# A fused adaLN block on one core: gate sums and weight preparation moved later, and the order of ScalarE and VectorE changed at the end of phase 1 and in the MLP's first pair

## The chip, the cores and the metric

The kernel runs on one core of a Trainium2 chip. The time is the device time of one execution in microseconds (us). The engines are named as in the profile: PE is TensorE's matmul, PEld its weight load, DVE VectorE, ACT ScalarE, POOL GpSimd, SP the engine that issues most loads and stores. A "phase" is a stage of the kernel, a "tile" 128 rows of x, a "pair" two tiles.

## The reference, cut to what matters

x has 2048 rows of 640 columns. Six vectors of 640 come from silu(c) @ w_mod.

```
mod = (_silu(c) @ w_mod).reshape(c.shape[0], 6, 1, -1)
sa, ca, ga, sb, cb, gb = (mod[:, 0], mod[:, 1], mod[:, 2], mod[:, 3], mod[:, 4], mod[:, 5])
h = _layernorm(x, axis=-1) * (1 + ca) + sa
x = x + ga * _A_ref(h, A_wqkv, A_w_phi, A_wo)
h = _layernorm(x, axis=-1) * (1 + cb) + sb
x = x + gb * _B_ref(h, B_w1, B_b1, B_w2, B_b2)
```

_A_ref is linear attention with 32 heads of 20 columns: q and k go through a small matrix per head and two softmaxes (of p and of -p), kv and z are sums of phi_k with v and with ones over all rows, the output is (phi_q kv) / (phi_q z) @ wo. _B_ref is relu(h @ w1 + b1)^2 @ w2 + b2 with 1728 hidden columns. All is float32.

## The kernel before, in words

Matrices are split into a high and a low part, and each product is three matmuls (high by high, high by low, low by high), so that nearly every tensor that PE reads needs a copy on ACT (the high part) and a subtraction on DVE (the low part).

**Phase 1** goes through 16 tiles of 128 rows, t = 0 to 15, in pairs j = t // 2. LayerNorm of a pair (ln_parts, L330) sums and squares on ACT, makes scale and bias on POOL, and scales x in place on ACT (L347: xb). t1 (L380) transposes scaled x on PE (ta, L356), applies 1 + ca and sa on ACT (hfa, L367), and splits the result into hT (high part ACT L368, low part DVE L87). proj (L393) multiplies hT with the weights of k, v or q into pk, pv, pq. spread (L424) takes each head's largest and smallest value on DVE (mx) and subtracts them, exps (L431) takes exponentials on ACT, k_norm (L435) sums a tile's heads on DVE (sk), inverts and scales; do_kv (L441) adds phi_k^T v up in PSUM (kvp). q_chain (L462) does the same for q: mxq, eq, the sums rs_q (L474), and a store of eq to DRAM (esp). A tile's steps end with SIDE[t] (L520), which spreads other preparation over the loop: the sums over the six gate vectors (stage, L311, loads a row block of w_mod, mac, L291, multiplies it with silu(c) and adds, four of the five with L295: wm), and prep_wo (L480), which loads the output weights, multiplies them by ga on DVE (rwo, L495) and splits them (wo, ACT L496, DVE L87).

In this loop (L697) PE's order is written by hand. The other engines' order comes from a scheduler, which may be told that an instruction goes behind another (issue_after). The last four tiles of q, and k and v of tiles 14 and 15, are postponed behind the loop; from there (L740 on) the order on PE, DVE, ACT and POOL is the order of the code, while SP's is still the scheduler's. mod_row (L324) adds the 128 partitions of a gate sum up with a matmul of ones (mr, L327) and copies it to all partitions (gb_b, L328). bb is b2 times gb. kvs, zb and kvd are copies of kvp, zb filled on ACT and DVE from matmuls z (L790).

**Phase 2** divides and projects. For each tile e_prod (L842) multiplies eq (read back from DRAM as el) with zb (scr), e_recip and e_scale make ezb on DVE; tr_e (L881) turns ezb on PE (te) and copies it on ACT (ept); num (L896) multiplies by kv; num_hi and num_lo copy the high part to ot, subtract it in PSUM with a negative identity, and copy the low part; do_wo multiplies by wo (pwo). Loads and stores go through SP's queue, in order, each waiting for its row of memory. Rows of 640 columns that are short-lived (loads of w_mod and wo, b2s, MLP weights) share five places, tag s1.

**The MLP** goes through eight pairs j and seven steps n, two blocks of hidden columns each: up makes relu(...)^2 in ft (ACT L1209, DVE L1210), split_a the parts ra (ACT L1233), down multiplies with w2 one step later (acc). The next pair's second LayerNorm is done in pieces (ln_pieces, L1438: sums L1443, squares L1448, POOL L1450 to L1452, scaling xm L1455), put in by layer at the steps that LN_AT0 names; prep converts weights (w, ACT L978, DVE L87) in between.

Of the kernel before, what the change touches and what calls it, by code (L numbers as in the profile page):

```python
# [17 lines left out]
D = 640  # L18
# [32 lines left out]
def kernel(  # L51
# [85 lines left out]
    def tp(name):  # L137
        return psA.tile([P, 512], F32, tag="tp", name=name)
# [179 lines left out]
    def mod_mac(part, *ks):  # L318
        for k, t in [(k, stage(part * D, k)) for k in ks]:
            with tc.issue_after(newest(ET_.DVE)):  # L320
                mac(t, t, k, MA.get(part))
            MA[part] = t

    def mod_row(part, dest, h):  # L324
        p = tp(f"mr{part}_{h}")
        c = slice(h * HALF, (h + 1) * HALF)
        nc.tensor.matmul(p[:, :HALF], ones, MA[part][:, c], start=True, stop=True)  # L327
        nc.scalar.activation(dest[:, c], p[:, :HALF], AF.Copy)  # L328
# [48 lines left out]
    def newest(engine):  # L377
        return next(i for i in reversed(nc.cur_bb.bb.instructions) if i.engine == engine)

    def t1(j, *ds, more=None):  # L380
        if 0 in ds:
            HT[j] = ht(f"hT{j}", j)
        p = tp(f"ta{j}_{ds[0]}")
        for k, d in enumerate(ds):
            t_in(XB[j], d, p[:, 256 * k : 256 * k + 256])
        if more:
            mod_turn(more[0], p[:, 256:], 4)
        for k, d in enumerate(ds):
            t_out(cols_a, HT[j], d, f"a{j}", p[:, 256 * k : 256 * k + 256])
        if more:  # L390
            mod_sum(*more)

# [111 lines left out]
    def biases():  # L504
        b2s.append(row("s1", "b2s"))
        nc.sync.dma_start(b2s[0], bass.AP(tensor=b2.tensor, offset=b2.offset, ap=[[0, P], [1, D]]))
        nc.sync.dma_start(b1_t, b1)

    def wo_weights(*gs):
        for g in gs:  # L510
            prep_wo(g, ga_b)
# [14 lines left out]
        7: lambda: mod_mac(2, 4),  # L526
        8: lambda: None,
        9: lambda: wo_weights(0, 1),
        10: lambda: wo_weights(2, 3),
        11: lambda: wo_weights(4, 5),  # L530
        12: lambda: (nc.vector.tensor_scalar(cols_b[:, 5:10], cols_b[:, 5:10], 1.0, None, op0=ALU.add), mod_mac(5, 0, 1, 2)),
        13: lambda: (mod_mac(5, 3, 4), biases()),
    }


# [161 lines left out]
    for t in range(2, NT - 2):  # L697
        j, i = divmod(t, 2)
        if i == 0 and j < NT // 2 - 2:
            load_x(j + 2)  # L700
        PK[t] = row("s2", f"k{t}")
        to_sb(proj("k", t), PK[t])
        if t == NT - 4:
            t1(j + 1, 0, 1)
        if t == 9:
            mod_row(2, ga_b, 1)
        norm = j + 1 if i == 0 and t < NT - 4 else j + 2 if t == NT - 5 else None
        if norm:
            parts = ln_parts(XB[norm], f"a{norm}")
            with tc.issue_after(newest(ET_.Activation)):  # L710
                next(parts)
        p = proj("v", t, (1, 0, lambda: t1(j + 1, 4)) if t == NT - 3 else None)
        if i == 0:
            do_kv(t - 2)
            do_kv(t - 1)
            if t in AFTER_KV:
                AFTER_KV[t]()
        v_out(t, p)
        if norm:
            next(parts)  # L720
        EK[t] = tok2("k", f"ek{t}")
        spread(PK[t], EK[t], f"k{t}")
        exps(EK[t])
        if norm:
            next(parts)
        if i and t < NT - 4:
            t1(j + 1, 2, 3)
        with tc.issue_after(newest(ET_.DVE)):
            k_norm(EK[t], t)
        if t < NT - POSTPONED:  # L730
            do_q(t, (1, 3, lambda: t1(j + 1, 4, more=LAST_COL.get(t))) if i else None)
            q_chain(t)
        if i == 0 and t < NT - 4:
            t1(j + 1, 0, 1)
        SIDE[t]()
# [14 lines left out]
        spread(PK[t], EK[t], f"k{t}")  # L750
    do_kv(ka - 2)
    do_kv(ka - 1)
    mod_row(5, gb_b, 0)
    exps(EK[ka])
    k_norm(EK[ka], ka)
    do_q(q0)
    mod_row(5, gb_b, 1)
    exps(EK[kb])
    k_norm(EK[kb], kb)
    do_v(ka)  # L760
    q_chain(q0, False)
    do_v(kb)
    exps(EQ[q0])
    nc.vector.tensor_tensor(bb, b2s[0], gb_b, op=ALU.mult)
    q_sums(q0)
    do_kv(ka)
    do_kv(kb)
    kvs = flat(tok2("w", "kvs"))
# [313 lines left out]
    load_e(4)  # L1082
    do_q(q0 + 3, (1, 8, lambda: tr_e(0, range(3))))
    tr_e(0, range(3, NG))
    num(0)
    num_hi(0)
    num_lo(0)
    e_prod(3)
    e_recip(2)
# [8 lines left out]
    for j in range(NB):  # L1098
        nxt = j + 1 < NB
        b, c = 2 * j + 5, 2 * j + 6  # L1100
        late_te = j == 0
        te_at = (0, 1) if 0 < j < 6 else (1, 2)
        if j == 4:
            load_x1(0)
        if j < 5:
            p_load()
        if j != 5:
            e_prod(b)
        e_recip(b - 1)
        e_scale(b - 1)  # L1110
        if j == 5:
            q_chain(KEPT + 3, False)
            add_x(0, 0, 1)
            ln0 = ln_parts(XM[0], "b0")
        load_e(b + 2)
        def te(at):
            for i, gs in enumerate((range(3), range(3, NG))):
                if nxt and not late_te and te_at[i] == at:
                    tr_e(j + 1, gs)

        do_wo(j, 0, 0)
        te(0)
        if j == 5:
            exps(EQ[KEPT + 3])
            q_sums(KEPT + 3)
            e_prod(b)
        do_wo(j, 0, 1)
        if j == 7:
            t2(0, 0)
            t2(0, 1)  # L1130
        te(1)
        if j == 5 or j == 6:
            next(ln0)
# [12 lines left out]
        if nxt:  # L1146
            if late_te:
                tr_e(j + 1, range(NG))
            num(j + 1)
            num_hi(j + 1)  # L1150
        do_wo(j, 1, 1, 0, 8)
        if j == 7:
            t2(0, 4)
        if not nxt:
            do_wo(j, 1, 1, 8, 16)
        if nxt:
            do_wo(j, 1, 1, 8, 11)
            num_lo(j + 1)
            do_wo(j, 1, 1, 11, 16)
        if j in SPREAD:  # L1160
            exps(EQ[KEPT + SPREAD[j]])
        load_e(c + 2)
        if j == 5:
            next(ln0)
        if 1 <= j < 6:
            p_hi()
        if j == 5:
            p_lo(4)
            p_load(4)
        if j == 6:  # L1170
            p_hi(4)
            p_lo(5)
            p_load(3)
        if j == 7:
            p_load(2)
# [304 lines left out]
    for j in range(NB):  # L1480
# [5 lines left out]
        for n in range(NP):  # L1486
# [66 lines left out]
                down(1)  # L1553
            if m == NP + 1:
                t_split(NP - 2)
            prep(next(PREPS, 0))
            if n == 0 and j:
                end(j - 1, "4", 1, L)
                end(j - 1, "x", 1, R)
            if n == (2 if j > PLAIN else 1 if j == PLAIN else 0) and j:  # L1560
                finish(j - 1, j >= PLAIN)
            layer(j + 1, 2 * n + 1)
            if 0 <= m < NP - 2:
                t_sums(m)
            if m == NP - 2:
# [69 lines left out]
```

## Time and profile before

| | us |
|---|---|
| median of 3 runs | 780.81 |
| lowest and highest run | 779.15, 781.12 |
| the profiled execution | 779.39 |
| its span, first to last instruction | 777.7 |
| PE busy in the span | 765.6 |
| DVE busy | 580.2 |
| ACT busy | 443.6 |
| POOL busy | 146.7 |

The rest of the profiled execution's time, 1.7 us, lies around the span. A line of a group or timeline reads: source line, engine, operation, out<-in by the program's names without numbers, shape, count; idle time of the engine in front of it stands in brackets, with what ended it ("<-ACT hT L368": an instruction of ACT that wrote hT). Matmuls overlap, so the distance between two starts tells more of PE's pace than a duration. Line numbers in the prediction are those of the kernel before.

### The profile page before, as it was taken

The page shows a single profiled execution, that of the slowest core. Times are in us where ns is not written, and L with a number is a line of the kernel's source. Part 1 is how long each engine was busy: PE and PEld are TensorE (multiplying, and loading weights), DVE is VectorE, ACT ScalarE, POOL GpSimd, SP SyncE. Part 2 cuts the span into 40 slices and gives each one's busy share as a digit, 9 for nine tenths or more (in the row PEclk, how much of TensorE's full clock was granted, in tenths as well). Part 3 has the DMA queues.
Part 4 walks back from the last instruction along what each step waited for, and adds up shares of the span by engine and source line. Part 5 has one row for each costly group of instructions (what it writes and reads, how often), then busy time and mean ns, then how long its engine had stood idle before and what let it go on. Part 6 is the DMA issues. An engine that isn't in the chain of part 4 may idle for free. (4 is left out here: it accounts for less than half of the span.)

```text
span 777.7 us, 15333 instructions
## 1 busy us (share of the span) xinstructions
PE 765.6 (98%) x5989; PEld 744.1 (96%) x5989; DVE 580.2 (75%) x1057; ACT 443.6 (57%) x995; POOL 146.7 (19%) x301
## 2 busy tenths in 40 slices
PE   9999999999899999999999999999999999999997
PEld 9999999999798988998899999999999999999997
DVE  6698897978898799986356667776767567585656
ACT  5766656666853355665876737546454645536331
POOL 3001101202000236532000101122221313213110
PEclk9999999999999999999999999999999999999999
DMA  8711432412343054323237446897666858667450
GB/s 330 294 68 68 136 102 70 168 68 82 135 141 120 23 181 151 105 76 111 85 125 266 137 168 232 283 326 238 191 199 209 234 179 260 188 190 209 122 178 35
DMA packets 50551, 126.03 MB, mean 162 GB/s; under 512 B 5991, under 2 KB 6759, under 8 KB 50479
## 3 DMA queue, kind: packets, MB, share of 16 engines
q1 hardware_dynamic: 33144, 83.99, 31.0%
q0 software_dynamic: 14752, 35.76, 16.4%
q10 hardware_dynamic: 2583, 5.30, 1.8%
q8 instruction: 47, 0.77, 0.4%
q14 instruction: 25, 0.20, 0.1%
HBM read 95.05 MB, written 29.88 MB: 161 GB/s over the span
## 5 line engine op out<-in xcount | busy, mean ns | idle before, releaser
L77 PE MATMUL up<-h,w 128*128 128x256 f32 x1640 | 206.5, 278 | 0.2 <-ACT ft L1209 0.2
L77 PEld LDWEIGHTS up<-h,w 128*128 128x128 f32 x1640 | 196.1, 188 | 0.3 <-ACT ft L1209 0.3
L1209 ACT ACTIVATE ft<-up,b_t 128x256 f32<-128x256 f32 x104 | 49.1, 472 | 113.8 <-PE up L77 113.2
L77 PE MATMUL acc<-w,ra 128*128 128x384 f32 x452 | 98.1, 336 | 0.6 <-ACT ra L1233 0.6
L1210 DVE TENSOR_TENSOR ft<-ft 128x256 f32<-128x256 f32 x104 | 44.1, 424 | 53.5 <-ACT ft L1209 51.8
L77 PE MATMUL pwo<-wo,ot 128*128 128x256 f32 (+3 forms) x512 | 81.1, 312 | 0.0
L77 PEld LDWEIGHTS pwo<-wo,ot 128*128 128x128 f32 (+1 forms) x512 | 75.0, 188 | 2.7 <-issue 2.7
L77 PE MATMUL pk<-wk,hT 128*128 128x384 f32 (+1 forms) x480 | 73.7, 309 | 2.5 <-DVE hT L87 1.9
L77 PE MATMUL pq<-wq,hT 128*128 128x384 f32 (+1 forms) x480 | 75.6, 312 | 0.0
L77 PEld LDWEIGHTS acc<-w,ra 128*128 128x128 f32 x452 | 72.6, 188 | 1.7 <-ACT ra L1233 0.8
L77 PEld LDWEIGHTS pk<-wk,hT 128*128 128x128 f32 x480 | 70.4, 188 | 4.0 <-DVE hT L87 2.3
L77 PE MATMUL pv<-wv,hT 128*128 128x384 f32 (+1 forms) x480 | 72.3, 308 | 0.0
L77 PEld LDWEIGHTS pq<-wq,hT 128*128 128x128 f32 x480 | 71.3, 188 | 0.9 <-issue 0.2
L77 PEld LDWEIGHTS pv<-wv,hT 128*128 128x128 f32 x480 | 70.3, 188 | 0.3
L87 DVE TENSOR_TENSOR ra<-ft,ra 128x384 fp32r<-128x384 f32 (+2 forms) x86 | 36.8, 449 | 32.8 <-ACT ra L1233 20.2
L77 PE MATMUL acc3x<-w,ra 128*128 128x256 f32 x248 | 42.4, 278 | 0.0
L1319 POOL DMA_DIRECT2D ring_a<-td_a x34 | 18.3, 538 | 123.7 <-PE acc L77 102.3
L1233 ACT ACTIVATE ra<-ft 128x384 fp32r<-128x384 f32 x48 | 25.3, 526 | 28.4 <-DVE ft L1210 22.4
L77 PEld LDWEIGHTS acc3x<-w,ra 128*128 128x128 f32 x248 | 39.8, 188 | 0.2 <-DVE ra L87 0.2
L437 DVE TENSOR_REDUCE sk<-ek 128x64 f32<-128x1280 f32 x16 | 23.7, 1482 | 16.0 <-ACT ek L432 13.4
L1224 DVE TENSOR_TENSOR ft<-ft 128x128 f32<-128x128 f32 x136 | 33.3, 286 | 1.2
L854 POOL TENSOR_TENSOR dn<-dn,rs_q 128x32 f32<-128x32 f32 x32 | 18.9, 592 | 74.0 <-DVE dn L848 73.8
(260 smaller groups left out, 1417.9 us busy)
## 6 DMA issues: line engine op xcount, KB each, us to landing
ring_c<-td_c POOLq DMA_DIRECT2D x34, 384.0 KB, 4.1
ring_a<-td_a POOLq DMA_DIRECT2D x34, 384.0 KB, 3.8
ring_b<-td_b POOLq DMA_DIRECT2D x34, 256.0 KB, 3.9
esp<-eq SPq DMA_DIRECT2D x12, 640.0 KB, 2.9
el<-esp SPq DMA_DIRECT2D x12, 640.0 KB, 3.8
rw<-in_w SPq DMA_DIRECT2D x23, 320.0 KB, 3.1
wm<-in_w_mod SPq DMA_DIRECT2D x20, 320.0 KB, 3.4
xb<-in_x SPq DMA_DIRECT2D x8, 640.0 KB, 3.9
```

The costliest lines, as they stand in the source:

```text
L77: nc.tensor.matmul(o, a, b, start=first and i == 0, stop=last and i == len(terms) - 1, skip_group_check=skip,)
L87: (eng or nc.vector).tensor_tensor(out_lo, full, hi.bitcast(F32), op=ALU.subtract)
L437: nc.vector.tensor_reduce(s, heads(flat(e)), axis=AX.X, op=ALU.add)
L854: nc.gpsimd.tensor_tensor(dn[:, s], dn[:, s], rs[:, 1 - s], op=ALU.mult)
L1209: nc.scalar.activation(r, p, AF.Relu, bias=b1_t[:, f : f + 1])
L1210: nc.vector.tensor_tensor(r, r, r, op=ALU.mult)
L1224: nc.vector.tensor_tensor(t[:, o], t[:, a], t[:, b], op=op)
L1233: nc.scalar.activation(a[:, 0, :3], t[:, :3], AF.Copy)
L1319: nc.gpsimd.dma_start(RING[j, n, r], TD[n][r].bitcast(F32R))
```

## The change: what it does

It has three parts.

1. In phase 1, the scaling of LayerNorm for the pair that is prepared in an odd tile (t = 11, pair 7) and q's chain of every odd tile are told to go behind the splitting of turned x (DONE holds the last ACT and the last DVE instruction of t1). Of the output weights, groups 3 to 5 move from tiles 10 and 11 to tiles 12 and 13.
2. The five loads and multiply-adds of the gate gb move from tiles 12 and 13 to behind the loop: all five loads are asked for at tile 13 (gb_load), the multiply-adds (gb_mac) stand one by one among the work of tiles 12, 14 and 15. The two halves of mod_row(5) move from there into the start of phase 2, with banks of its PSUM pool. The load of b2 goes behind the last multiply-add, and bb's product into round j = 5 of phase 2.
3. In the MLP, at pair 0, step 3, the two squares of the next pair's LayerNorm go ahead of two weight parts.

```diff
-    def mod_row(part, dest, h):
-        p = tp(f"mr{part}_{h}")
+    def mod_row(part, dest, h, p=None):
+        p = p or tp(f"mr{part}_{h}")
...
             t_out(cols_a, HT[j], d, f"a{j}", p[:, 256 * k : 256 * k + 256])
+        DONE[:] = newest(ET_.Activation), newest(ET_.DVE)
...
+    def gb_load():
+        GB.extend((k, stage(5 * D, k)) for k in range(NC))
         nc.sync.dma_start(b1_t, b1)
+
+    def gb_mac(n=1):
+        for _ in range(n):
+            k, t = GB.pop(0)
+            mac(t, t, k, MA.get(5))
+            MA[5] = t
...
         9: lambda: wo_weights(0, 1),
-        10: lambda: wo_weights(2, 3),
-        11: lambda: wo_weights(4, 5),
-        12: lambda: (nc.vector.tensor_scalar(cols_b[:, 5:10], cols_b[:, 5:10], 1.0, None, op0=ALU.add), mod_mac(5, 0, 1, 2)),
-        13: lambda: (mod_mac(5, 3, 4), biases()),
+        10: lambda: wo_weights(2),
+        11: lambda: None,
+        12: lambda: (nc.vector.tensor_scalar(cols_b[:, 5:10], cols_b[:, 5:10], 1.0, None, op0=ALU.add), wo_weights(3, 4)),
+        13: lambda: (wo_weights(5), gb_load()),
...
-        if norm:
+        if norm and not i:
             next(parts)
...
-            q_chain(t)
+            if norm and i:
+                with tc.issue_after(newest(ET_.Activation)), tc.issue_after(DONE[0]):
+                    next(parts)
+            if i:
+                with tc.issue_after(DONE[1]):
+                    q_chain(t)
+            else:
+                q_chain(t)
...
-    mod_row(5, gb_b, 0)
+    gb_mac()
     exps(EK[ka])
     k_norm(EK[ka], ka)
     do_q(q0)
-    mod_row(5, gb_b, 1)
+    gb_mac()
     exps(EK[kb])
     k_norm(EK[kb], kb)
     do_v(ka)
     q_chain(q0, False)
+    gb_mac()
     do_v(kb)
     exps(EQ[q0])
-    nc.vector.tensor_tensor(bb, b2s[0], gb_b, op=ALU.mult)
     q_sums(q0)
+    gb_mac(2)
+    biases()
...
     tr_e(0, range(3, NG))
+    mod_row(5, gb_b, 0, bank("mr5_0"))
     num(0)
     num_hi(0)
+    mod_row(5, gb_b, 1, bank("mr5_1"))
     num_lo(0)
...
             add_x(0, 0, 1)
+            nc.vector.tensor_tensor(bb, b2s[0], gb_b, op=ALU.mult)
             ln0 = ln_parts(XM[0], "b0")
...
+            ahead = (j, n) == (0, 3)
+            if ahead:
+                layer(j + 1, 2 * n + 1)
             prep(next(PREPS, 0))
...
-            layer(j + 1, 2 * n + 1)
+            if not ahead:
+                layer(j + 1, 2 * n + 1)
```

What stands where in the built programs, at three places. In these rows hT6 is turned x of pair 6 (read by tiles 12 and 13), the number behind a name its tile, and the last number only a buffer's.

First, ACT in tile 11, from the copies of turned x on. Before:

```order
L496 ACTIVATE wo3_2404<-rwo3_2400 128x640
L433 ACTIVATE ek11_2492<-ek11_2492 128x640
L347 ACTIVATE xb7_2204<-xb7_2204,nba7_2445,sqa7_2444 128x640 x2
L422 ACTIVATE q11_2561<-pq11_0_2519 128x384
L368 ACTIVATE hT6_2378<-hfa6_2_2507 128x256
L368 ACTIVATE hT6_2378<-hfa6_3_2511 128x256
```

ACT at the same place, now:

```order
L436 ACTIVATE ek11_2484<-ek11_2484 128x640
L425 ACTIVATE q11_2551<-pq11_0_2509 128x384
L368 ACTIVATE hT6_2378<-hfa6_2_2497 128x256
L368 ACTIVATE hT6_2378<-hfa6_3_2501 128x256
L305 ACTIVATE mt4_2302<-ta6_4_2529 128x128
L367 ACTIVATE hfa6_4_2534<-ta6_4_2529,cols_a_100 128x256
L425 ACTIVATE q11_2551<-pq11_1_2510 128x256
L368 ACTIVATE hT6_2378<-hfa6_4_2534 128x256
L347 ACTIVATE xb7_2204<-xb7_2204,nba7_2437,sqa7_2436 128x640 x2
```

The output weight wo3 is gone from here, and the scaling xb7 stands behind the last part of hT6.

DVE at the same place, before:

```order
L495 TENSOR_TENSOR rwo3_2400<-rwo3_2400,ga_b_226 128x640
L429 TENSOR_TENSOR ek11_2492<-k11_2408,mxk11_2493 128x640
L474 TENSOR_REDUCE rs_q_106<-eq10_2368 128x64
L87 TENSOR_TENSOR wo3_2404<-rwo3_2400,wo3_2404 128x640
L87 TENSOR_TENSOR hT6_2378<-hfa6_2_2507,hT6_2378 128x256
L87 TENSOR_TENSOR hT6_2378<-hfa6_3_2511,hT6_2378 128x256
L437 TENSOR_REDUCE sk11_2515<-ek11_2492 128x64
L426 TENSOR_REDUCE mxq11_2565<-q11_2561 128x32
L427 TENSOR_REDUCE mxq11_2565<-q11_2561 128x32
L87 TENSOR_TENSOR hT6_2378<-hfa6_4_2544,hT6_2378 128x256
```

And now:

```order
L432 TENSOR_TENSOR ek11_2484<-k11_2400,mxk11_2485 128x640
L477 TENSOR_REDUCE rs_q_106<-eq10_2368 128x64
L87 TENSOR_TENSOR hT6_2378<-hfa6_2_2497,hT6_2378 128x256
L87 TENSOR_TENSOR hT6_2378<-hfa6_3_2501,hT6_2378 128x256
L440 TENSOR_REDUCE sk11_2505<-ek11_2484 128x64
L87 TENSOR_TENSOR hT6_2378<-hfa6_4_2534,hT6_2378 128x256
L309 TENSOR_REDUCE cols_b_101<-mt4_2302 128x5
L429 TENSOR_REDUCE mxq11_2557<-q11_2551 128x32
```

Both rows of wo3 are gone from here, and q's reductions mxq11 stand behind the low part of hT6's column 4.

Second, DVE ahead of zb, at the end of phase 1 (eq12 is q of tile 12, wm3200_k row block k of the gate sum gb). Before:

```order
L426 TENSOR_REDUCE mxq12_3031<-eq12_2835 128x32
L427 TENSOR_REDUCE mxq12_3031<-eq12_2835 128x32
L429 TENSOR_TENSOR eq12_2835<-eq12_2835,mxq12_3031 128x640 x2
L764 TENSOR_TENSOR bb_103<-b2s_2829,gb_b_102 128x640
L474 TENSOR_REDUCE rs_q_106<-eq12_2835 128x64
L798 COPY zb_3106<-z0_0_3119 128x4x60
```

And now:

```order
L432 TENSOR_TENSOR eq12_2828<-eq12_2828,mxq12_3020 128x640 x2
L295 SCALAR_TENSOR_TENSOR wm3200_2_2818<-wm3200_2_2818,cs_178,wm3200_1_2816 128x640
L477 TENSOR_REDUCE rs_q_106<-eq12_2828 128x64
L295 SCALAR_TENSOR_TENSOR wm3200_3_2820<-wm3200_3_2820,cs_178,wm3200_2_2818 128x640
L295 SCALAR_TENSOR_TENSOR wm3200_4_2822<-wm3200_4_2822,cs_178,wm3200_3_2820 128x640
L821 COPY zb_3099<-z0_0_3112 128x4x60
```

bb is gone from here, and three multiply-adds of the gate sum came in, two of them between rs_q and the first copy to zb.

Third, ACT in the MLP at pair 0, step 3 (xx and sqb1 belong to the next pair's LayerNorm, w2_8 and w1_13 are weight parts). Before:

```order
L1239 ACTIVATE ra0_3_5142<-ft0_3_5101 128x128
L978 ACTIVATE w2_8_5030<-rw2_8_5031 128x640
L978 ACTIVATE w1_13_5033<-rw1_13_5034 128x640
L1448 ACTIVATE xx1_0_4992,sqb1_5083<-xm1_4939,smb1_5082 128x640
L1448 ACTIVATE xx1_1_4993,sqb1_5083<-xm1_4939,smb1_5082 128x640
L1209 ACTIVATE ft0_4_5190<-up_4825,b1_t_99 128x2x128
```

And now:

```order
L1265 ACTIVATE ra0_3_5142<-ft0_3_5101 128x128
L1474 ACTIVATE xx1_0_4992,sqb1_5083<-xm1_4939,smb1_5082 128x640
L1474 ACTIVATE xx1_1_4993,sqb1_5083<-xm1_4939,smb1_5082 128x640
L1001 ACTIVATE w2_8_5030<-rw2_8_5031 128x640
L1001 ACTIVATE w1_13_5033<-rw1_13_5034 128x640
L1235 ACTIVATE ft0_4_5190<-up_4825,b1_t_99 128x2x128
```

The squares and the weight parts have changed places; nothing else moved.

More of the change, by code (lines that the diff above doesn't have):

```diff
@@ L378, in newest @@
         return next(i for i in reversed(nc.cur_bb.bb.instructions) if i.engine == engine)
+    DONE = []
     def t1(j, *ds, more=None):
@@ L506, in biases @@
         nc.sync.dma_start(b2s[0], bass.AP(tensor=b2.tensor, offset=b2.offset, ap=[[0, P], [1, D]]))
+    GB = []
+    def gb_load():
+        GB.extend((k, stage(5 * D, k)) for k in range(NC))
         nc.sync.dma_start(b1_t, b1)
+    def gb_mac(n=1):
[3 more added lines that the diff above has]
+            MA[5] = t
     def wo_weights(*gs):
```

## The prediction

> **What bounds the kernel now.** I read the page's first part, then the waits of PE, then the timelines of PE, DVE and ACT around each wait.
>
> ```profile
> span 777.7 us, 15333 instructions
> PE 765.6 (98%) x5989; PEld 744.1 (96%) x5989; DVE 580.2 (75%) x1057; ACT 443.6 (57%) x995; POOL 146.7 (19%) x301
> ```
>
> PE (TensorE's matmuls) is busy for 765.6 of 777.7 us, so about 12 us at most can be won without removing matmuls. The waits of PE say where whole stops lie; the numbers are the total, the count and the longest, in us.
>
> ```profile
> PE pk L77 <- DVE hT L87: 1.9, 1, 1.9
> PE mr L327 <- DVE wm L295: 1.6, 1, 1.6
> ...
> PE ta L356 <- ACT hfa L367: 0.6, 1, 0.6
> PE acc L77 <- ACT ra L1233: 0.6, 1, 0.6
> ```
>
> Each happens once, so each is a single place in the program. The change touches pk (k's projection of tile 12, which reads turned x), mr (the gate sum gb) and acc (the MLP's first pair). The 0.6 of ta should stay, since ACT's order up to the hfa that it waits for is unchanged.
>
> **1. Turned x at the end of phase 1.** PE first; a row is start, duration, instruction, count, and in brackets the idle time before it.
>
> ```profile
> 203.81 1.20 PE L77 MATMUL pk<-wk,hT 128*128 128x384 f32 x6
> 205.56 2.13 PE L77 MATMUL pk<-wk,hT 128*128 128x384 f32 x8 [0.55 <-ACT hT L368]
> 209.54 2.17 PE L77 MATMUL pk<-wk,hT 128*128 128x384 f32 x16 [1.85 <-DVE hT L87]
> 211.55 0.60 PE L356 MATMUL ta<-ident,xb 128*128 128x128 f32 x4
> ```
>
> For comparison PE at the next tile, whose turned x is ready:
>
> ```profile
> 219.34 4.62 PE L77 MATMUL pk<-wk,hT 128*128 128x384 f32 x30
> 223.80 2.76 PE L77 MATMUL pv<-wv,hT 128*128 128x384 f32 x15
> ```
>
> There the same 30 matmuls take 223.80 - 219.34 = 4.46 us from start to start. For tile 12 they took 211.55 - 203.81 = 7.74. So 3.28 us are lost, more than the two brackets (2.40): the eight matmuls of 2.13 us hide a further stop.
>
> [...]
>
> Now DVE and ACT at this place.
>
> ```profile
> 205.54 0.76 DVE L87 TENSOR_TENSOR hT<-hfa,hT 128x256 fp32r<-128x256 f32 x2 [2.10 <-ACT hT L368]
> 206.22 1.48 DVE L437 TENSOR_REDUCE sk<-ek 128x64 f32<-128x1280 f32 x1
> 207.62 0.81 DVE L426 TENSOR_REDUCE mxq<-q 128x32 f32<-128x640 f32 x1
> ```
>
> ```profile
> 201.82 0.76 ACT L496 ACTIVATE wo<-rwo 128x640 fp32r<-128x640 f32 x1
> 202.45 0.76 ACT L433 ACTIVATE ek<-ek 128x640 f32<-128x640 f32 x1
> 203.08 1.75 ACT L347 ACTIVATE xb<-xb,nba,sqa 128x640 f32<-128x640 f32 x2
> 204.70 0.51 ACT L422 ACTIVATE q<-pq 128x384 f32<-128x384 f32 x1
> 205.07 0.74 ACT L368 ACTIVATE hT<-hfa 128x256 fp32r<-128x256 f32 x2
> ...
> 206.56 0.46 ACT L368 ACTIVATE hT<-hfa 128x256 fp32r<-128x256 f32 x1
> ```
>
> In the new order wo (0.63 to the next start) and xb (1.62) stand behind hT on ACT. So the high parts of columns 2 and 3 start at 205.07 - 2.25 = 202.82, and that of column 4 ends at 206.56 + 0.46 - 2.25 = 204.77. DVE starts its low parts 0.47 after the high ones, as now: 203.29. The reduce sk (1.40 to the next start) still comes between, the two mxq no longer, so column 4's low part starts at 203.29 + 0.68 + 1.40 = 205.37 and is there by 205.8. PE needs it for the 15th matmul of pk, near 203.81 + 2.4 = 206.2 (the row of pv shows 15 such matmuls in 2.76, the length of the last among it, so the 15th starts some 2.4 in). **Both waits go, with 0.4 us to spare: -3.3 us.** Should the margin fail, PE waits for one DVE instruction again, at most sk's 1.4.
>
> What is queued behind the moved steps: on ACT, behind xb, the copies of k and the hfa of tile pair 7. xb now ends near 204.7 + 1.75 = 206.5, and its reader, the transposes ta, comes at 203.81 + 4.46 = 208.3. On DVE the scaling of tile 11's ek stands behind q's chain; its rows added up in the new order, each by its distance from start to start, let it end near 213.5, and PE reaches that tile's kv near 214.4. Both hold, by 1 to 2 us.
>
> **2. The gate sum.**
>
> ```profile
> 241.22 0.81 PE L327 MATMUL mr<-wm,ones 128*128 128x320 f32 x2 [1.60 <-DVE wm L295]
> 241.62 4.79 PE L77 MATMUL pq<-wq,hT 128*128 128x384 f32 x30
> ```
>
> Without mr here, pq starts 1.60 + 0.40 = 2.0 us earlier, and the second half of gb, 4.6 us later, takes away another 0.3 to 0.4: **-2.3 us**.
>
> The multiply-adds do not vanish. The last two now stand on DVE ahead of zb:
>
> ```profile
> 240.30 0.87 DVE L295 SCALAR_TENSOR_TENSOR wm<-wm,cs,wm 128x640 f32<-128x640 f32 x1
> ```
>
> ```profile
> 261.43 0.85 DVE L798 COPY zb<-z 128x240 f32<-128x240 f32 x3 [2.31 <-ACT zb L800]
> ...
> 262.58 1.49 DVE L846 TENSOR_TENSOR scr<-el,zb 128x1280 f32<-128x1280 f32 x1
> ```
>
> Two of 0.87 fit into the idle 2.31 ahead of zb with 0.6 to spare, so I charge nothing. Without that cover zb, and the transposes te behind it, come up to 1.7 us late.
>
> The two matmul groups of mr run again at the start of phase 2, among te, num and the first pwo, and their copies gb_b stand on ACT ahead of the parts of ot:
>
> ```profile
> 242.06 0.44 ACT L328 ACTIVATE gb_b<-mr 128x320 f32<-128x320 f32 x1 [4.49 <-PE mr L327]
> ```
>
> ```profile
> 280.39 4.82 PE L77 MATMUL pwo<-wo,ot 128*128 128x384 f32 x32
> ```
>
> PE pays two times 0.3 to 0.4. ACT is a link there (num, then ot's high part, then the subtraction, then its low part, then pwo), so the copies may cost too. Bounds: 0.6 if both copies are hidden, 0.8 + 0.9 = 1.7 if both hold pwo up in full; less than 0.6 is excluded, as PE has the same matmuls to run. I take **+0.8 us**, near the lower end: the first copy can run while PE is in num. pwo would then start near 280.4 - 3.3 - 2.3 + 0.8 = 275.6.
>
> The product bb moves into round 5 of phase 2, where DVE idles for 4.93 us before its next instruction, so its 0.8 us cost nothing:
>
> ```profile
> 363.80 1.49 DVE L474 TENSOR_REDUCE rs_q<-eq 128x64 f32<-128x1280 f32 x1 [4.93 <-ACT eq L433]
> ```
>
> Its row b2s stays occupied until then, so the load of one MLP weight is issued behind bb; its first reader on ACT comes a whole round later, so I charge nothing for that either.
>
> **3. The MLP's first pair.**
>
> ```profile
> 424.14 0.72 ACT L978 ACTIVATE w<-rw 128x640 fp32r<-128x640 f32 x1
> ...
> 426.39 0.81 ACT L1448 ACTIVATE xx<-xm,smb 128x640 f32<-128x640 f32 x1
> ...
> 430.05 0.92 ACT L1455 ACTIVATE xm<-xm,nbb,sqb 128x640 f32<-128x640 f32 x1 [0.95 <-POOL nbb L1452]
> ```
>
> The squares (L1448) start at 424.14 instead of 426.39, so POOL's nbb is there 2.25 us earlier and the 0.95 ahead of xm is gone. The two weight parts behind them end where the squares ended, so nothing between is late. What follows xm up to ra comes 0.95 earlier, and PE waits 0.6 for ra: **-0.6 us**, 0.3 to spare.
>
> **Sum.** -3.3 - 2.3 + 0.8 - 0.6 = -5.4 us. The profiled execution took 779.39 us (span 777.7 and 1.7 around it) and would become 774.0. It lies 1.4 under the median of 780.81; the three runs shown, 779.15 to 781.12, have a mean of 780.1. I go from there, between the two: **774.7 us**. The bounds of the terms alone reach from -3.1 (sk's 1.4 comes back, the copies cost 0.9 more) to -6.2 (mr costs 0.6, and ta's 0.6 goes as well).
>
> **The rivals.**
>
> *A new wait in the place of the old.* DVE has nearly the same work in a stretch that shrinks:
>
> ```profile
> 196.00:262.00 66.00, 61.28 (x491) 57.95 (x490) 55.85 (x72) 34.77 (x86) 2.61 (x5) 1.00 0.37 122
> ```
>
> Of 66 us DVE is busy for 55.85 (the third engine). With 5.6 us less time and bb gone, some 5 us of idle time are left; that speaks against a DVE bound, its fixed order, in which one late row holds all behind it, speaks for one. The price: the multiply-adds' 1.7 ahead of zb, or sk's 1.4, with or without the copies' 0.9: 776.1 to 777.3.
>
> *The change does only half of what it says:* hT's low part is still held on DVE, the 3.3 stay, and only the gate sum and the MLP act: 780.1 - 2.1 = 778.0. The new order speaks against it, since q's reductions stand behind the low part of column 4.
>
> *Slower: the load queue.*
>
> ```profile
> 238.49 1.53 SPq L836 DMA_DIRECT2D el<-esp  x2
> ```
>
> ```profile
> el<-esp SPq DMA_DIRECT2D x12, 640.0 KB, 3.8
> ```
>
> The loads of el stand on SP behind the load of the last gate row, which in the new program waits for wo's last low part. So far they are issued at 238.5 and used by scr at 262.58. With the change their use moves to about 257; such a load takes 3.8 us from issue to landing, so PE is held once they are issued after 253, and the kernel is slower than before once it is after 258.6. By DVE's rows wo's last part should end near 233. A slip to 260 gives 781.5.
>
> **How the numbers follow.** Forecast 0.64, new wait 0.20, half of the change 0.10, load queue 0.06. The range 772.9 to 778.3 holds the forecast with the scatter of the runs, and the first two rivals. A measurement of this kernel can tell about 0.3%, 2.3 us, from no change, so faster means below 778.5: the forecast, the first rival and a part of the second, 0.86. Within 0.3% are the rest of the second and small slips, 0.09; slower 0.05.
>
> **What would show it.** Right: pk of tile 12 lasts 4.5 us up to ta and has no bracket; no wait mr <- wm; pq follows kvp at once; DVE still idles ahead of zb; pwo starts near 275.6; acc <- ra is gone. Wrong: a bracket te <- DVE ezb, one of pk <- DVE hT, one of more than 0.5 at pwo <- ACT ot, or scr waiting for a load.

## The result, and the profile after

The changed kernel takes 773.97 us (median of 6 runs, 773.74 to 774.41), the kernel before 780.66 in the same comparison (median of 6, 779.15 to 781.12). The ratio is 0.9918 with a 95% interval of 0.9905 to 0.993. The profiled execution took 773.97 us with a span of 772.2, against 779.39 and 777.7 before.

The top of the page, and below it the two largest of PE's waits that are left (total, count, longest, in us); the other two are of 0.3 and 0.2:

```profile
span 772.2 us, 15334 instructions
PE 764.6 (99%) x5989; PEld 744.1 (96%) x5989; DVE 580.3 (75%) x1057; ACT 443.3 (57%) x995; POOL 145.5 (19%) x301
```

```profile
PE warm L623 <- POOL bdc L154: 1.1, 1, 1.1
PE ta L356 <- ACT hfa L367: 0.6, 1, 0.6
```

The three waits that the change touches (pk, mr, acc) are gone; the 0.6 of ta stayed, as forecast. The engines do the same work as before in 5.5 us less span.

**Turned x.** PE from the transposes of column 4 on:

```profile
202.78 0.44 PE L356 MATMUL ta<-ident,xb 128*128 128x128 f32 x2 [0.62 <-ACT hfa L367]
...
204.54 4.47 PE L77 MATMUL pk<-wk,hT 128*128 128x384 f32 x30
208.85 0.60 PE L356 MATMUL ta<-ident,xb 128*128 128x128 f32 x4
```

One row of 30 matmuls stands where three rows with two brackets stood: 208.85 - 204.54 = 4.31 us instead of 7.74, so 3.43 are won. DVE at the same place:

```profile
204.07 0.76 DVE L87 TENSOR_TENSOR hT<-hfa,hT 128x256 fp32r<-128x256 f32 x2 [1.80 <-ACT hT L368]
204.75 1.48 DVE L440 TENSOR_REDUCE sk<-ek 128x64 f32<-128x1280 f32 x1
206.15 0.41 DVE L87 TENSOR_TENSOR hT<-hfa,hT 128x256 fp32r<-128x256 f32 x1
```

The last row is column 4's low part. This execution is 0.78 us later from the start-up on (ta of pair 6 starts at 198.54, before at 197.76). Less that, the low part starts at 205.37, the forecast to the hundredth.

**The gate sum's old place.** PE behind kvp of tiles 12 and 13, now and (second fence) before; the row is start, duration, instruction, count:

```profile
234.31 2.54 PE L449 MATMUL kvp<-ek,vt 128*64 128x120 f32 x44
236.78 4.64 PE L77 MATMUL pq<-wq,hT 128*128 128x384 f32 x30
241.26 8.76 PE L77 MATMUL pv<-wv,hT 128*128 128x384 f32 x60
249.95 2.54 PE L449 MATMUL kvp<-ek,vt 128*64 128x120 f32 x44
```

```profile
237.08 2.54 PE L446 MATMUL kvp<-ek,vt 128*64 128x120 f32 x44
...
246.25 0.70 PE L327 MATMUL mr<-wm,ones 128*128 128x320 f32 x2
246.55 9.18 PE L77 MATMUL pv<-wv,hT 128*128 128x384 f32 x60
255.66 2.54 PE L446 MATMUL kvp<-ek,vt 128*64 128x120 f32 x44
```

From kvp to pq (before at 241.62) it is 2.47 us instead of 4.54 (-2.07), from pq to pv 4.48 instead of 4.93 (-0.45), and the 60 matmuls of pv take 8.69 instead of 9.11 (-0.42), which the forecast doesn't have.

**Ahead of zb.** DVE's last two multiply-adds and its margin:

```profile
253.33 1.79 DVE L295 SCALAR_TENSOR_TENSOR wm<-wm,cs,wm 128x640 f32<-128x640 f32 x2
255.72 0.85 DVE L821 COPY zb<-z 128x240 f32<-128x240 f32 x3 [0.59 <-ACT zb L823]
```

The forecast was 0.6 to spare; it is 0.59.

**mr's new place.** PE from the last te to the first pwo:

```profile
269.46 1.25 PE L913 MATMUL te<-ident,ezb 128*120 128x128 f32 x10
270.75 0.81 PE L327 MATMUL mr<-wm,ones 128*128 128x320 f32 x2
271.48 1.08 PE L77 MATMUL numa<-ept,kvd 120*64 120x256 f32 x8
272.67 1.08 PE L77 MATMUL numb<-ept,kvd 120*64 120x256 f32 x8
...
274.55 0.81 PE L327 MATMUL mr<-wm,ones 128*128 128x320 f32 x2
...
275.90 7.79 PE L77 MATMUL pwo<-wo,ot 128*128 128x384 f32 x48
```

The first te (267.29) is 5.70 us ahead of its time before, pwo (275.90 against 280.39) only 4.49: mr's return costs 1.21 us. The first half alone takes 0.73 to the next start, and numb comes 1.19 behind numa, where in round 1 of the same trace it is 0.92. The second half costs little: from numc to pwo it is 2.31 us instead of 2.13.

**The MLP's first pair**, PE now and (second fence) before:

```profile
425.55 1.86 PE L77 MATMUL up<-h,w 128*128 128x256 f32 x15
427.25 0.76 PE L77 MATMUL acc<-w,ra 128*128 128x384 f32 x3
...
429.08 0.60 PE L356 MATMUL tb<-ident,xm 128*128 128x128 f32 x4
```

```profile
429.91 1.86 PE L77 MATMUL up<-h,w 128*128 128x256 f32 x15
432.41 1.04 PE L77 MATMUL acc<-w,ra 128*128 128x384 f32 x3 [0.63 <-ACT ra L1233]
...
434.51 0.60 PE L356 MATMUL tb<-ident,xm 128*128 128x128 f32 x4
```

From up to tb it is 3.53 instead of 4.60 us: 1.07 won, of which the bracket shows 0.63.

The parts sum to -3.43 - 2.07 - 0.45 - 0.42 + 1.21 - 1.07 = -6.23. With the 0.78 of the later start-up that is -5.45, and the spans differ by 5.5. The medians differ by 6.7, which is more than the one profiled execution of each can explain; the last part of the experiments, on the clock, is about that.

### The profile page after: what moved, and what is told of

It is laid out like the page before. It is cut to its first block, busy times and chain, and to the rows that moved or that the text cites. A ratio compares the mean times of both kernels' runs of the same rounds, so it can differ in the third digit from the quotient of the medians.

```text
span 772.2 us, 15334 instructions
## 1 busy us (share of the span) xinstructions
PE 764.6 (99%) x5989; PEld 744.1 (96%) x5989; DVE 580.3 (75%) x1057; ACT 443.3 (57%) x995; POOL 145.5 (19%) x301
## 4 chain that ended last, share of the span: by engine, by line
PE 94%; ACT 2%; DVE 1%; DMA 1%; issue 1%; POOL 0%; SPq 0%; ACTq 0%; POOLq 0%
PE up L77 24%; PE acc L77 17%; PE pwo L77 10%; PE pk L77 8%; PE pq L77 8%; PE pv L77 8%; PE acc3x L77 5%; PE kvp L449 2%; PE te L913 2%; PE tb L356 1%; PE numa L77 1%; PE numb L77 1%; PE numc L77 1%; PE ta L356 1%; PE foldk L279 1%; PE foldq L279 1%
## 5 line engine op out<-in xcount | busy, mean ns | idle before, releaser
L477 DVE TENSOR_REDUCE rs_q<-eq 128x64 f32<-128x1280 f32 x16 | 23.7, 1479 | 9.6 <-ACT eq L436 9.6
```

The source lines that it names most:

```text
L477: nc.vector.tensor_reduce(s, heads(flat(e)), axis=AX.X, op=ALU.add)
```

## Experiments

The theory is the forecast's: three stops that don't depend on each other, each worth what PE's starts show. The rivals are that they are coupled (what PE wins it waits for later, above all on DVE), or that one part brings all.

**One part alone, on top of the kernel before.** *order_only*: LayerNorm's scaling and q's chain behind turned x, everything else as before.

```
+    DONE = []
...
+        DONE[:] = newest(ET_.Activation), newest(ET_.DVE)
...
-        if norm:
+        if norm and not i:
             next(parts)
...
-            q_chain(t)
+            if norm and i:
+                with tc.issue_after(newest(ET_.Activation)), tc.issue_after(DONE[0]):
+                    next(parts)
+            if i:
+                with tc.issue_after(DONE[1]):
+                    q_chain(t)
+            else:
+                q_chain(t)
```

> The kernel before with one part of the change: LayerNorm's scaling of xb and q's chain stand behind turned x; the output weights and the gate sum stay where they were, so wo's copy (0.63 us) still stands ahead of hT on ACT. Theory (three independent stops): columns 2 and 3 go out 0.63 us later than in the changed kernel, column 4's low part is there about 0.2 to 0.3 us late for PE's 15th matmul, so pk of tile 12 takes 4.6 to 4.8 us from its start to the next transposes (7.74 before, 4.31 in the changed kernel); the time falls by 3.0 to 3.3 us, to about 777.5. Rival (the order alone doesn't free hT, the moved output weights do it): pk keeps over 6.5 us and the time falls by less than 1.3. Rival (the stops are coupled: PE that comes 3.3 us sooner waits longer for the gate sum): the wait of mr for wm grows from 1.6 to about 4.9 us and the time does not fall at all.

*xb_only*: the same with `q_chain(t)` left as it was (without the last five lines), so that q's chain stays where it was.

> The kernel before with LayerNorm's scaling of xb behind turned x and nothing else: q's two reductions (0.73 us each from start to start) stand ahead of column 4's low part again. Theory: ACT gives the high parts about 1.6 us sooner, but DVE holds column 4's low part back by two reductions; pk of tile 12 takes about 6.0 us, the time falls by 1.5 to 1.9, to about 779. Rival (the scaling on ACT is all of it): pk 4.6 to 4.8 and the same gain as with q's chain moved too. Rival (DVE is all of it): pk stays over 7 us, no gain.

*gate_only*: the changed kernel with these lines and the MLP's taken back.

> The kernel before with the output weights and the gate sum later (their loads, the multiply-adds behind kvp, mr in phase 2, bb in round 5), turned x and the MLP as before. Theory: from kvp of tiles 12 and 13 to pq of tile 12 PE wins 2.07 us, 0.45 where mr's second half stood, and loses 1.21 at the start of phase 2: -1.3, and -1.7 if the 0.42 us by which the two pv got shorter in the changed kernel come from mr's copies too; time about 779. The wait of 1.9 at pk <- hT stays or shrinks by at most 0.6, since wo's copy no longer stands ahead of hT on ACT. Rival (the 0.42 come from another part of the change): pv x60 takes 9.18 us again and the sum is -1.3. Rival (without the earlier PE, DVE's margin ahead of zb is another): zb shows no idle time ahead of it and te starts late.

*mlp_only*: the kernel before with the lines on `ahead` in the MLP's loop.

> The kernel before with LayerNorm's squares ahead of the weight parts in the MLP's first pair, nothing else. Theory: the wait acc <- ra (0.6) goes and the next up comes 0.6 to 1.1 us sooner after the first than before (11.79 us from up to up before); time 780.0. That is less than the times can tell, so the trace decides. Rival (the wait moves to another place of the same pair): a new bracket at up or acc, and the distance from up to up stays 11.8.

| kernel | us, median (runs) | ratio to before, 95% interval | pk of tile 12, start to next ta |
|---|---|---|---|
| order_only | 777.10 (5) | 0.9952 (0.9938 to 0.9967) | 4.67 |
| xb_only | 778.39 (9) | 0.9969 (0.9958 to 0.9981) | 6.12 |
| gate_only | 778.82 (9) | 0.9971 (0.9958 to 0.9985) | 7.13 |
| mlp_only | 779.72 (12) | 0.9981 (0.997 to 0.9992) | 8.91 |

The kernel before had 780.99 (24 runs) beside them. The times of order_only and xb_only fell by 3.9 and 2.6 us, more than the 3.0 to 3.3 and 1.5 to 1.9 that were expected; from ta of pair 6 to pwo their traces show 2.79 and 1.62. The rest fits the clock told below. PE of order_only, then of xb_only:

```profile
204.59 4.84 PE L77 MATMUL pk<-wk,hT 128*128 128x384 f32 x30
209.26 0.60 PE L356 MATMUL ta<-ident,xb 128*128 128x128 f32 x4
...
236.39 1.35 PE L449 MATMUL kvp<-ek,vt 128*64 128x120 f32 x22 [0.23 <-DVE ek L442]
239.35 0.81 PE L327 MATMUL mr<-wm,ones 128*128 128x320 f32 x2 [1.60 <-DVE wm L295]
```

```profile
204.11 2.59 PE L77 MATMUL pk<-wk,hT 128*128 128x384 f32 x14
208.22 2.17 PE L77 MATMUL pk<-wk,hT 128*128 128x384 f32 x16 [1.53 <-DVE hT L87]
210.23 0.60 PE L356 MATMUL ta<-ident,xb 128*128 128x128 f32 x4
```

The order frees hT, in three shares: the scaling on ACT brings 7.74 - 6.12 = 1.62 us, q's two reductions behind column 4 another 1.45, the output weights' copy behind hT 0.36 more (4.31 in the changed kernel). Both expected sizes held (4.6 to 4.8 and 6.0). order_only's pk has no bracket on PE; its weight loads (PEld) show the stop: in the 2 us from 206, around the 15th, they are busy for 1.60 and PE for 1.92, so they idle for 0.40. The coupling is there, but small: with pk shorter a stop of 0.23 at kvp <- DVE ek appears that the kernel before doesn't have, and mr's wait is still 1.6, since DVE, which it waits for, came sooner too.

In gate_only pv takes 8.69 us (243.80 to 252.49), so the 0.42 came with this part of the change; from ta behind pk to pwo it is 67.07 instead of 68.84 us, -1.77, the theory's -1.7. Ahead of zb DVE has the same 0.59 us to spare there, so the rival on DVE's margin falls. In mlp_only up to tb takes 3.55 us, 0.02 over the changed kernel, and the wait acc <- ra is gone; a wait of 0.69 us of an acc for a load at 526.60, some 90 us later, stands in this one execution only. The clock told below disturbs the times and the pk of mlp_only (8.91).

**Is DVE the next bound?** *dve3* adds work that nobody needs ahead of zb:

```
     gb_mac(2)
+    for _ in range(3):
+        nc.vector.tensor_tensor(bb, ga_b, ga_b, op=ALU.mult)
```

> The changed kernel with three more instructions on DVE ahead of zb (each a product of 128x640, 0.73 us from start to start, into a tile that nobody reads before round 5): 2.2 us of work that the kernel doesn't need, for the price of a DVE that is late there. Theory: zb has 0.59 us to spare ahead of it and nothing behind it, so zb and the transposes te come 1.6 us later, and the time is 1.6 us over the changed kernel, 775.6. Rival (idle time behind zb takes it in, so that the first rival of the forecast was no danger): te less than 0.7 us late and less than 0.7 us in the time. Rival (te is late already): 2.2 in full.

It took 775.59 us (5 runs, 775.51 to 775.98). PE at te:

```profile
267.32 0.38 PE L915 MATMUL te<-ident,ezb 128*120 128x128 f32 x2
269.31 1.31 PE L915 MATMUL te<-ident,ezb 128*120 128x128 f32 x10 [1.61 <-DVE ezb L895]
```

Of 2.19 us, 0.58 vanish in the margin of zb and 1.61 hold PE; the time grows by 1.6. So the forecast's first rival is a real danger, and 0.6 us is all that keeps it away.

*hfa_early* goes the other way: it takes away PE's remaining wait in front of the same DVE.

```
-        exps(EK[t])
+        if t != 11:
+            exps(EK[t])
...
-        with tc.issue_after(newest(ET_.DVE)):
-            k_norm(EK[t], t)
+        if t == 11:
+            with tc.issue_after(newest(ET_.Activation)):
+                exps(EK[t])
+        else:
+            with tc.issue_after(newest(ET_.DVE)):
+                k_norm(EK[t], t)
...
+            if t == 11:
+                with tc.issue_after(DONE[1]):
+                    k_norm(EK[t], t)
...
-                with tc.issue_after(DONE[1]):
+                with tc.issue_after(newest(ET_.DVE) if t == 11 else DONE[1]):
                     q_chain(t)
```

> The changed kernel with, in tile 11, the two hfa and the two high parts of columns 2 and 3 ahead of the two exponentials of k on ACT, and the reduction sk, the reciprocal and the scaling of ek on DVE behind column 4's low part, with q's chain behind them. Theory (the wait ta <- hfa of 0.62 us comes from one exponential, 0.63 us, ahead of hfa, and the margin at hT was held by sk): the bracket ta <- ACT hfa goes, column 4's low part follows its high part without sk between, pk of tile 12 stays at 4.3 to 4.5 us; from the transposes ahead of pq of tile 11 to those behind pk of tile 12 it takes 9.7 instead of 10.31 us, in all -0.6. Rival (ACT and DVE are full there, and what is moved back is missed later): a bracket at kvp <- DVE ek or ta <- ACT hfa elsewhere, and kvp of tiles 12 and 13 starts no sooner. Rival (PE is now held by column 4 through ACT): pk over 4.7.

It took 773.92 us (4 runs, 773.37 to 774.26), the time of the changed kernel.

```profile
202.09 0.44 PE L356 MATMUL ta<-ident,xb 128*128 128x128 f32 x2
...
235.33 1.35 PE L449 MATMUL kvp<-ek,vt 128*64 128x120 f32 x22 [0.23 <-DVE ek L442]
...
267.05 1.73 PE L921 MATMUL te<-ident,ezb 128*120 128x128 f32 x12
```

The bracket at ta is gone, and from ta (198.47) to the ta behind pk (208.19) it takes 9.72 instead of 10.31 us, as the theory had it. The theory on the time fell all the same, and its rival held: 0.42 come back at kvp (2.89 to pq instead of 2.47) and 0.22 in the first te. But the edit changed DVE's order as well. The scaling of tile 13's ek (L442), which in the changed kernel ends at 231.15, more than 3 us ahead of that kvp, ends here at 235.18, behind reductions and subtractions for another tile's k, and DVE has nothing left to spare ahead of zb. So the gain is lost against this order of DVE. That PE can win nothing more ahead of kvp and te is not shown, and mr_later_hook below speaks against it.

**What does mr's return cost, and where should it stand?** *mr_later* puts the two halves behind the first two groups of pwo:

```
-    mod_row(5, gb_b, 0, bank("mr5_0"))
     num(0)
     num_hi(0)
-    mod_row(5, gb_b, 1, bank("mr5_1"))
...
         do_wo(j, 0, 0)
+        if j == 0:
+            mod_row(5, gb_b, 0, bank("mr5_0"))
...
         do_wo(j, 0, 1)
+        if j == 0:
+            mod_row(5, gb_b, 1, bank("mr5_1"))
```

> The changed kernel with the two halves of mr behind the first and the second group of pwo in round 0 of phase 2, where ACT is idle, in place of their place among te, num and the first pwo. Theory (mr's return cost 1.21 us because ACT's copies and PE's two groups stand in the chain num, high part, subtraction, low part, pwo): pwo starts 1.2 us sooner after te than in the changed kernel (3.9 instead of 5.15 us from the last te's end to pwo), mr then costs 0.3 to 0.4 each among the pwo; in all -0.4 to -0.6, to about 773.5, which the trace can tell and the times hardly. Rival (mr costs what its matmuls cost, wherever it stands): the same time within 0.2 from te to the next te. Rival (its copies hold the next num's banks or pwo's copies): a new bracket at te or num in round 1, slower than the changed kernel.

773.92 us (4 runs, 773.64 to 774.18): nothing won. From the last te to pwo it is 5.19 us instead of 6.44, and each half costs 0.30 among the pwo, as expected. Those two and pwo's 48 matmuls, which take 0.31 longer, leave 0.35 of the 1.25 at the first te of round 1 (13.71 us from te to te, 14.06 in the changed kernel), and up to the MLP's first up 0.46 are lost again:

```profile
394.05 5.39 PE L77 MATMUL up<-h,w 128*128 128x256 f32 x45 [0.31 <-ACT hfb L367]
```

It starts 1.50 us behind the start of the last group of pwo, in the changed kernel 1.04. In the program the up waits there for the reader of column 4 of the last transposes, in the changed kernel for that of column 2: the psum banks go round in the order of their requests, and now column 4's transposes land on the one that up takes. *mr_tp* gives the second half the bank of numc (`mod_row(5, gb_b, 1)` without `bank`), and *best_a* is mr_tp with hfa_early.

> hfa_early and mr_later together, with the second half of mr in the bank that numc uses, so that the MLP's first up doesn't share a bank with the last transposes ahead of it (in mr_later up waited 0.31 us for the reader of that bank and started 1.50 instead of 1.04 us after the last pwo). Theory (each is a stop of its own): -0.6 from hfa, -0.3 from mr, none of it lost at up: -0.9 against the changed kernel, 773.1. Rival (mr's gain is lost at up for another reason): up starts 1.5 us after the last pwo again, and the time is that of hfa_early.

> best_a without what hfa_early moves: only mr's two halves in round 0 of phase 2, the second in the bank that numc uses. Theory (in hfa_early the 0.6 us that PE won ahead of pk were given back at kvp and te, because DVE sets the start of te): from the first hfa on nothing is lost, the time is that of best_a, 773.4 to 773.6, and up starts 1.0 us after the last pwo. Rival (hfa's gain is in best_a's time): 773.9 to 774.1.

best_a was expected at 773.1 and took 773.40 us (4 runs, 773.31 to 773.41; ratio to before 0.9898, 0.9882 to 0.9915), mr_tp 773.65 (5 runs, 772.77 to 774.37; 0.9905, 0.9889 to 0.992). In both, up starts 1.03 to 1.04 us behind the last pwo and has no bracket. best_a lies under every run of the changed kernel, by 0.6 us in the median: the fastest of the study, by little; mr_tp's runs cover what its theory and its rival expected. Whether hfa_early has a share in it the times don't tell. The traces say a little more: from ta of pair 6 to the MLP's first up it is 195.84 us in the changed kernel, 195.89 in hfa_early, 195.55 in mr_tp and 195.47 in best_a. So moving mr wins 0.3 up to there, and hfa_early 0.1 at most. From that up to the end single executions differ by as much (377.8 to 378.1 us).

*mr_later_hook* is mr_later with the transposes of column 4 three matmuls later in tile 11 (`6 if t == 11 else 3`).

> As mr_later, and in tile 11 the transposes of column 4 stand behind three more matmuls of pq, so that PE doesn't wait 0.62 us for hfa. Theory (by the forecast, 0.4 us were to spare at column 4's low part): the bracket ta <- ACT hfa falls from 0.62 to 0.2 or less, pk of tile 12 starts 0.45 to 0.6 sooner and holds all but about 0.2 of it: 0.4 us in all. Rival (the margin at hT is nothing): the same time comes back as a bracket pk <- DVE hT of 0.4 to 0.6, and the transposes behind pk start when they did.

774.18 us (4 runs, 773.53 to 774.63). The bracket at ta falls to 0.33, pk starts 0.33 sooner, counted from the first ta of pair 6 (5.67 us instead of 6.00), and takes 4.47 instead of 4.31. So 0.16 of it is lost: the margin at column 4's low part is about 0.2 us, not the forecast's 0.4. The rest is kept: from ta to the first te it is 68.56 us, in mr_later 68.76, and DVE still has 0.59 to spare ahead of zb. The times can't tell 0.2 us.

*act_copy* looks for the 0.42 us of pv.

```
     do_q(q0)
+    nc.scalar.activation(bb[:, :HALF], ga_b[:, :HALF], AF.Copy)
     gb_mac()
```

> The changed kernel with one more copy on ACT of 128x320 behind those of pq of tile 12, where the second gb_b stood before (it writes a tile that nobody reads before round 5), without its matmuls on PE. It asks where the 0.42 us come from by which the two pv became shorter. Theory (ACT's copy delays the reads that free pv's banks): pv x60 takes 9.0 us or more from its start to kvp, as before. Rival (the mr matmuls themselves, with the weights they load between two projections, slow PE down): it stays at 8.7.

773.95 us (1 run); pv takes 8.69 (241.10 to 249.79). ACT's copy isn't the cause. That it is the two mr matmuls is not shown by this; it stays open.

**The clock.** Each timed execution lists the mean clock that PE was granted. Of the 49 executions of the kernel before that ran beside these experiments, 37 had 0.996 or 0.997 and 781.3 us in the mean, 12 had 0.998 or more and 779.6 (the ranges overlap: 779.17 to 782.15 and 779.26 to 780.44). The six of the changed kernel all had 0.998 or more. mlp_only falls in the same two groups (7 at 780.2, 5 at 778.1), and its profiled execution shows what happens. A row is the stretch, its length, PE's busy time and instructions, those of PEld, DVE, ACT and POOL, the granted clock, DMA share and GB/s:

```profile
208.00:210.00 2.00, 0.56 (x2) 0.25 (x2) 2.00 (x4) 0.00 (x0) 0.00 (x0) 1.00 0.09 33
210.00:212.00 2.00, 1.57 (x9) 1.57 (x10) 2.00 (x5) 0.49 (x1) 0.00 (x0) 0.78 0.00 0
212.00:214.00 2.00, 2.00 (x12) 2.00 (x11) 2.00 (x5) 0.93 (x2) 0.00 (x0) 0.50 0.56 164
214.00:216.00 2.00, 2.00 (x12) 2.00 (x12) 2.00 (x3) 1.53 (x4) 0.00 (x0) 0.87 0.00 0
```

Behind the stop in pk the clock falls, to 0.50 over the whole third row. At that depth the last three rows make (0.22 + 0.50 + 0.13) x 2 / 0.5 = 3.4 us, which loses 1.7. In the profiled execution of the kernel before the same stop stands without it (1.00 in every row from 202 to 216 us), so that its slower executions have this fall is inferred from mlp_only and from the size, 1.7 us. *pe_stop* makes the stop again in the changed kernel:

```
-            t_out(cols_a, HT[j], d, f"a{j}", p[:, 256 * k : 256 * k + 256])
+            if (j, d) == (NT // 2 - 2, 4):
+                with tc.issue_after(newest(ET_.DVE)):
+                    for _ in range(1):
+                        nc.vector.tensor_tensor(bb, ga_b, ga_b, op=ALU.mult)
+                with tc.issue_after(newest(ET_.DVE)):
+                    t_out(cols_a, HT[j], d, f"a{j}", p[:, 256 * k : 256 * k + 256])
+            else:
+                t_out(cols_a, HT[j], d, f"a{j}", p[:, 256 * k : 256 * k + 256])
```

> The changed kernel with column 4's low part of turned x behind the reciprocal and the scaling of tile 11's ek and one more product on DVE (0.6 + 1.4 + 0.73 us), so that PE stops once in pk of tile 12 for about 2.7 us. In the kernels so far whose pk stopped for 1.8 us or more (the kernel before, the squares alone, the gate sum alone) the executions fall in two groups: a granted clock of 0.996 or 0.997 and about 1.7 us more, or 0.998 and 0.999; with a stop of 1.5 or none the clock was 0.998 or more, but for one execution. Theory (the stop itself makes the clock fall right behind it): with 2.7 us nearly all executions have 0.997 or less, and the time is 2.7 + 1.7 over the changed kernel, about 778.4; the profiled one shows a stretch of a few us with a granted clock well below 1 behind the stop. Rival (the clock has nothing to do with the stop): the clock stays at 0.998 to 1.0 and the time is 776.7.

It took 778.13 us (5 runs, 777.66 to 778.54), with 0.996 or 0.997 in four of five; the fifth, with 0.998, took 777.66, where the rival had 776.7. PE, and the clock:

```profile
204.11 2.59 PE L77 MATMUL pk<-wk,hT 128*128 128x384 f32 x14
209.00 3.74 PE L77 MATMUL pk<-wk,hT 128*128 128x384 f32 x16 [2.30 <-DVE hT L87]
212.55 0.63 PE L356 MATMUL ta<-ident,xb 128*128 128x128 f32 x4
```

```profile
208.00:210.00 2.00, 1.00 (x5) 1.00 (x6) 2.00 (x4) 0.42 (x1) 0.00 (x0) 0.80 0.00 0
210.00:212.00 2.00, 2.00 (x11) 2.00 (x11) 2.00 (x5) 0.07 (x1) 0.00 (x0) 0.50 0.56 156
212.00:214.00 2.00, 2.00 (x14) 2.00 (x14) 2.00 (x3) 1.17 (x3) 0.00 (x0) 0.85 0.02 8
```

pk takes 8.44 us, 4.13 more than in the changed kernel: 2.6 for the stop, and 1.5 because the 16 matmuls behind it take 3.55 to the next start (2.01 in xb_only). The time rose by 4.2. So the stop that was put in brings the fall with it, right behind it: here a bracket of 2.3 us costs 4.

## Why the prediction was right

**Turned x, -3.3:** measured -3.43. The places on ACT and DVE came out as worked out, and it was right to count by starts: PE's brackets hold 2.40 of it, so the same term counted by brackets would have been 1.0 short. The weight loads show the stop nearly whole. PEld in the kernel before, at pk of tile 12:

```profile
205.56 0.30 PEld L77 LDWEIGHTS pk<-wk,hT 128*128 128x128 f32 x2 [0.88 <-ACT hT L368]
206.02 0.65 PEld L77 LDWEIGHTS pk<-wk,hT 128*128 128x128 f32 x4 [0.16 <-DVE hT L87]
207.07 0.30 PEld L77 LDWEIGHTS pk<-wk,hT 128*128 128x128 f32 x2 [0.40 <-ACT hT L368]
209.54 1.97 PEld L77 LDWEIGHTS pk<-wk,hT 128*128 128x128 f32 x16 [2.17 <-DVE hT L87]
```

These brackets add up to 3.61 us, and to 1.13 (0.83 and 0.30) at the MLP's acc, where 3.43 and 1.07 were won. Over the span PEld's idle time fell by 5.5 us (33.6 to 28.1), as the span did, and PE's by 4.5 (12.1 to 7.6). So the 12 us of idle PE are no firm bound of what can be won: 1.03 us of pk's 3.43 lay in rows that count as busy.

**Gate sum, -2.3:** measured -2.52 (2.07 + 0.45), and 0.42 more in pv that the forecast lacks; gate_only shows that they come with this part, the cause is open. Some 0.17 of them may be chance: mlp_only, edited in the MLP alone, has 8.94 where the kernel before has 9.11.

**mr's return, +0.8:** measured +1.21, inside the bounds of 0.6 to 1.7, but taken too near their lower end. The first copy does run while PE is in num (272.52), as forecast; what was mis-sized is the first half's place ahead of numa. From the last te to numc it is 4.13 us instead of 3.06, so that this half costs 1.07 instead of 0.3 to 0.4, and the second 0.18 (1.25 in all, counted from the last te). ACT, which has the last ept to copy, holds numb there (its weight load waits 0.56 us for it). Among the pwo, where ACT is idle (1.79 and 1.34 us ahead of its copies of pwo in the changed kernel), a half costs 0.30 (mr_later), and pwo's 48 matmuls took 0.31 more in that run.

**MLP's first pair, -0.6:** measured -1.07. The mechanism is the forecast's; the size was read off the bracket (0.63), though the same text had just shown for pk that a bracket is less than the stop. By starts (4.60 from up to tb, against 3.42 from up to up in the step ahead of it) it would have been 1.2.

**The sum, -5.4 on the profiled execution:** 774.0 was forecast for it, 773.97 came. That it is so close is luck: 0.78 of later start-up and 0.4 of mr stand against 1.2 too little in the MLP, pv, the gate sum and turned x. The terms alone came to -6.23, the far end of the bounds (-3.1 to -6.2). pwo's start (275.90 against 275.6) is such a case too: without the later start-up it is 275.12. Over all profiled kernels, which do the same work up to there, ta of pair 6 starts between 197.76 and 198.94, and the kernel before was the earliest.

**From the profile to the median, 774.0 to 774.7:** this step failed. The forecast took the scatter of the kernel before (779.15 to 781.12) for something that the changed kernel would have as well, and added half of it. By the experiments it goes with the granted clock, 781.3 us in the mean at 0.996 or 0.997 and 779.6 at 0.998 or more; that the fall behind the stop makes the difference is inferred, as no trace of the kernel before shows it. By that, without the fall 779.6 becomes 774.0 (-5.6), and the 1.7 that were lost in three of four executions (37 of 49) go too.

**The rivals.** DVE late ahead of zb didn't come true, by the 0.59 us that were forecast; dve3 shows what it costs once they are used up. hT free only by half: refuted by the single row of pk. The load queue: in the changed kernel the loads of el are issued at 235.72 and read at 256.87; nothing waits.

## What to carry to other kernels

Price a stop by the distance between PE's starts against the same work elsewhere, not by PE's bracket, which showed 2.40 of 3.43 us in pk and 0.63 of 1.07 in the MLP; the brackets of the weight loads came within 0.2 of both. Before removing a wait of one engine, look how far ahead of its own next deadline the engine behind it is: here DVE had 0.6 us to spare ahead of zb, and 2.2 us of work put there cost 1.6. When a kernel's times scatter in two groups, compare the granted clock of each execution before adding the scatter to a forecast: in the two traces that show the fall, behind brackets of 1.86 and 2.30 us, it cost 1.5 to 1.7 us more.

## What the hardware did that was not expected

The granted clock fell to a half for about 3.4 us behind a single stop of PE. With stops of 1.5 to 1.6 us (order_only, xb_only, dve3) the mean clock was 0.998 or more in 18 of 19 executions, and without them (the changed kernel and its other variants) in all 28. With one of 1.84 (gate_only) it was 0.997 in 4 of 9, with one of 2.30 (pe_stop) 0.997 or less in 4 of 5, and with 0.55 and 1.85 within 5 us (mlp_only 0.59 and 1.86) in 37 of 49 of the kernel before and 7 of 12 of mlp_only. The fall itself is seen in two traces, of mlp_only and pe_stop. They agree in its depth (0.50) and, at that depth, in its length, 3.4 us: (0.22 + 0.50 + 0.13) x 2 / 0.5 and (0.20 + 0.50 + 0.15) x 2 / 0.5. A gap of 2.30 us was enough in pe_stop's trace, and by the mean clock one of 1.84 in some executions of gate_only, whose own trace has no fall. With the same stop some executions show the lower mean clock and others don't, and what decides it is not shown.

PE's matmuls without any bracket don't always run at the same pace: 60 of pv took 9.11 (kernel before, xb_only), 8.94 (order_only, mlp_only) or 8.69 us (changed kernel, gate_only) at a granted clock of 1.00, and no run here shows why.
